# A linear-attention kernel feeding a SwiGLU block: diagonal blocks of the first group in 64x32 tiles, and joins over four array tiles in place of two

## The chip, the cores and the metric

The kernel runs on one core of one Trainium2 chip. The metric is the device time of one execution in microseconds (us); the time before is the median of three. A core has five engines that run side by side, each through its own queue in program order: TensorE (PE; matrix products, with a separate weight-load instruction, PEld), VectorE (DVE), ScalarE (ACT), GpSimd (POOL) and SyncE (SP, which here issues loads and stores). They wait for one another through semaphores. Data lies in SBUF, 128 partitions wide; PE writes its results into PSUM, and DVE or ACT copy them out.

## The reference, cut to what matters

```python
# q, k, v: (4, 8, 768, 48), beta: (4, 8, 768), all float32
k_n = k / (np.linalg.norm(k, axis=-1, keepdims=True) + 1e-06)
state = zeros((B, H, D, D))
for t in range(S):
    y[:, :, t] = q[:, :, t] @ state                  # per batch and head
    v_old = k_n[:, :, t] @ state
    state = state + beta_t * outer(k_n[:, :, t], v[:, :, t] - v_old)
x = y.transpose(0, 2, 1, 3).reshape(3072, 384)       # tokens, heads * head_dim
g, val = x @ w_gate, x @ w_val                       # (384, 1536) each
out = (g * sigmoid(g) * val) @ w_out                 # (1536, 384)
```

The recurrence over 768 steps is done in 12 chunks of 64 steps. In a chunk, the corrections of the steps on one another form a lower triangular system of 64 unknowns for each of the 32 (batch, head) pairs, made of the gram matrix of the chunk's keys and of beta. The kernel inverts that triangle. It treats two chunks at a time, called a group: group 0 is chunks 0 and 1. The two 32x32 diagonal blocks of every triangle are inverted on DVE by substitution, all 64 triangles of a group at once, one of the 128 blocks in each partition. The lower left block of the inverse is then a product of three 32x32 matrices, made on PE: this is the join.

## The kernel before: the parts that the change touches

Cuts are marked with `# ...`. C is 64 (steps in a chunk), R is 32, HH is 16 (heads side by side in a partition half), NB is 2, NJ is 4. All products are in float32; every float32 matmul is two records (a weight load and a matmul each) in the trace.

The gram matrix of a chunk, with its copies from PSUM to `a_sb`; the transposition of its diagonal blocks into `mb`; the substitution:

```python
def gram_steps(c, of_q, tag=None, copies=(nc.vector.tensor_copy,) * 2):
    xt = (qt if of_q else kt)[c]
    p_g = banks("p_g", tag or ("py" if of_q else "px"))
    p_v = [p.rearrange("p (bp j i) -> p bp j i", bp=NB, j=NJ) for p in p_g]
    for bp, j, par, b, _ in every():
        nc.tensor.matmul(
            p_v[par][half_of(b if of_q else b ^ par), bp, j],
            kt[c][half_of(par), bp, j, b],
            xt[half_of(par), bp, j, b],
        )
    if of_q:
        p_sb[c] = work.tile([128, 2, NB, NJ, C], FP32, name="p_sb", bufs=2)
    elif c % 2 == 0:
        a = work.tile([128, C * 2 * HH], FP32, name="a_sb")
        a_sb[c // 2] = (
            a.rearrange("p (i c h) -> p c h i", c=2, h=HH)
            if c == 0
            else a.rearrange("p (c h i) -> p c h i", c=2, h=HH)
        )
        a_of[c // 2] = a
    yield
    for par in range(2):
        p_h = p_g[par].rearrange("p (h i) -> p h i", i=C)
        if of_q:
            # ... masked product to p_sb
        else:
            at = slice(par * HH // 2, (par + 1) * HH // 2)
            copies[par](a_sb[c // 2][:, c % 2, at], p_h)
    yield
# ...
def turn(out, in_):
    nc.vector.transpose(out(slice(0, 128), 1), in_(slice(0, 128), 1))
    yield
    for rows in (slice(0, 32), slice(64, 96)):
        nc.vector.transpose(out(rows, 0), in_(rows, 0))
        yield
# ...
def scale_m(mb, m, b):
    zb = work.tile([128, R, R], FP32, name="zb", bufs=1)
    nc.gpsimd.memset(zb, 0.0)
    nc.gpsimd.tensor_copy(zb.rearrange("p k i -> p (k i)")[:, 0 : R * R : R + 1], b)
    nb = work.tile([128, R], FP32, name="nb", bufs=1)
    nc.vector.tensor_scalar_mul(nb, b, -1.0)
    for out, in_ in m:
        nc.vector.tensor_tensor(
            out=mb[:, out],
            in0=in_,
            in1=nb[:, None, :].to_broadcast([128, in_.shape[1], R]),
            op=ALU.mult,
        )
    return zb
def substitute(mb, zb):
    for j in range(R - 1):
        m = R - 1 - j
        tmp = work.tile([128, 256], FP32, name="tmp", bufs=1)
        t_v = tmp[:, 0 : (j + 1) * m].rearrange("p (k i) -> p k i", i=m)
        nc.vector.tensor_tensor(
            out=t_v,
            in0=zb[:, 0 : j + 1, j : j + 1].to_broadcast([128, j + 1, m]),
            in1=mb[:, j : j + 1, j + 1 : R].to_broadcast([128, j + 1, m]),
            op=ALU.mult,
        )
        nc.vector.tensor_tensor(
            out=zb[:, 0 : j + 1, j + 1 : R],
            in0=zb[:, 0 : j + 1, j + 1 : R],
            in1=t_v,
            op=ALU.add,
        )
        yield
```

The norms of the keys come as `n_t` from two powers on POOL; `first_n` turns them into factors, and `divide_beta` applies them twice to beta:

```python
def first_n():
    n = n_t[0].rearrange("p c h -> p (c h)")
    nc.vector.tensor_scalar_add(n, n, 1e-6)
    r_n = work.tile([128, R], FP32, name="r_n", tag="n_b", bufs=1)
    nc.vector.reciprocal(r_n, n)
    r_b = work.tile([128, R], FP32, name="r_b", tag="nb", bufs=1)
    nc.vector.transpose(r_b, r_n)
    return r_b
def divide_beta(g, r_n):
    for _ in range(2):
        nc.vector.tensor_tensor(
            out=beta_b[:, g], in0=beta_b[:, g], in1=r_n, op=ALU.mult
        )
```

After the substitution `late_z` writes the inverted blocks into `zt` and, turned, into `d_t`; `join_late` then makes the missing block. It is used for groups 0 and 1; later groups use another function, `join`, whose products are spread over four tiles of the array. `QUADS[n]` is the n-th quarter of the 128 partitions. The tile of the array that a matmul occupies follows from the partitions of its operands (rows) and of its result (columns).

```python
def late_z(g, zb):
    nc.vector.transpose(
        ztp[g % ZB].rearrange("p c h i -> p i (c h)")[:, R:C],
        zb.rearrange("p k i -> p i k"),
    )
    yield
    z_late[g] = work.tile([128, R, 2 * HH], FP32, name="d_t", tag="p_sb", bufs=2)
    nc.vector.transpose(z_late[g], zb)
    yield
def join_late(g, c, tags):
    zt, a, d_t = ztp[g % ZB], a_sb[g], z_late[g]
    p_j = banks("p_j", tags[0])[0].rearrange("p (h i) -> p h i", i=R)
    for h in range(HH):
        for s in range(2):
            hi, lo = QUADS[2 * s][0], QUADS[2 * s + 1][0]
            nc.tensor.matmul(p_j[hi, h], a[lo, c, h, 0:R], zt[lo, c, h, R:C])
    t2 = work.tile([128, HH, R], FP32, name="t2", tag="tmp", bufs=1)
    for s in range(2):
        hi = QUADS[2 * s][0]
        nc.scalar.mul(t2[hi], p_j[hi], -1.0)
    yield
    p_j = recur(ps_pair("p_j", tags[1]), C)
    for of_d in (True, False):
        for h in range(HH):
            par, bp, j = h // (NB * NJ), h // NJ % NB, h % NJ
            for s in range(2):
                hi = QUADS[2 * s][0]
                nc.tensor.matmul(
                    p_j[hi, par, bp, j, 0:R] if of_d else p_j[hi, par, bp, j, R:C],
                    d_t[hi, :, HH * c + h],
                    ident[hi, hi] if of_d else t2[hi, h],
                )
    zt_v = zt[:, c].rearrange("p (par bp j) i -> p par bp j i", par=2, bp=NB)
    for bp in range(NB):
        for hi in (QUADS[0][0], QUADS[2][0]):
            nc.scalar.copy(
                zt_v[hi, :, bp].rearrange("p par j i -> p par (j i)"),
                p_j[hi, :, bp].rearrange("p par j i -> p par (j i)"),
            )
    yield
```

The start of the program, in its order, which is the order of each engine's queue:

```python
# ... loads of k, beta, the first weights; norms(0), norms(1)
copy_a, copy_v = nc.scalar.copy, nc.vector.tensor_copy
turned(0, False)
turned(1, False, "py")
gram(0, False)
gram(1, False, "py", (copy_a, copy_v))
mb = new_mb()
a_v = a_of[0].rearrange("p (i m) -> p i m", i=C)
for _ in turn(
    lambda rows, half: mb[rows],
    lambda rows, half: a_v[rows, R * half : R * half + R],
):
    pass
r_b = first_n()
copy_v(beta_b, beta_s.rearrange("p (g r) -> p g r", g=NG)[:, :, 0:R])
for n in range(12, 17):
    stage(n)
load_v(1)
divide_beta(0, r_b)
zb = scale_m(mb, [(slice(0, R), mb)], beta_b[:, 0])
nc.gpsimd.memset(ztp[0], 0.0)
turned(0, True, "ffn")
turned(2, False, "px")
turned(3, False, "py")
first_q = gram_steps(0, True, "ffn")
next(first_q)
gram(2, False, "px", (copy_a, copy_a))
gram(3, False, "py", (copy_a, copy_a))
for n, _ in enumerate(substitute(mb, zb)):
    if n == R // 2:
        for i in range(4):
            power_step(i)
m_1 = turned_m(1, "ffn")
scale_v_heads(0)
turned(1, True, "px")
for _ in late_z(0, zb):
    pass
mb = new_mb()
mbs.append(mb)
first_join = join_late(0, 0, ("px", "py"))
next(first_join)
converts(2)
next(first_q)
next(first_join)
nc.scalar.copy(mb[:, m_1[0][0]], m_1[0][1])
step("advance", advance, 0)
converts(2)
step("advance", advance, 0)
nc.scalar.copy(mb[:, m_1[1][0]], m_1[1][1])
converts(2)
step("advance", advance, 0)
converts(2)
step("advance", advance, 0)
converts(2)
second_inverse.append(invert(1))
# ... then the gate and value products of chunk 0, with the second
# join of group 0 (join_late(0, 1, ...)) between the first of them
```

`converts` are the weights' conversions from float64 words to float32 on DVE and ACT, in pieces as they are loaded; `advance(0)` is the use of the inverted triangles for chunk 0, up to the input of the SwiGLU block.

## Time and profile before

| | |
|---|---|
| time, three runs | 747.40 (median), 746.36 to 749.35 us |
| span of the profiled run | 748.4 us |
| PE busy | 706.7 us, 10004 matmul records |
| DVE busy | 475.2 us, 981 instructions |
| ACT busy | 149.5 us |
| POOL busy | 67.4 us |
| first product of the SwiGLU block (L800) starts | 67.57 us |
| substitution of group 0 (L515, L521) | 23.63 to 47.6 us |
| joins of groups 0 and 1 (L568, L580) | at 49.8, 73.9, 180.3 and 198.8 us |

How to read it: a row of the timeline or of the groups gives the engine, the line of the kernel, the operation, then the tile written and the tiles read, the shape, and how often. Idle time ahead of an instruction stands in brackets with what ended it; "issue" there means that the engine waited for nothing that the profile shows. PEclk is the share of full clock that PE was granted. Busy shares of the whole span mix stages with different limits, so stages are read one by one.

### The profile page before, as it was taken

The page shows a single profiled execution, that of the slowest core. Times are in us where ns is not written, and L with a number is a line of the kernel's source. Part 1 is how long each engine was busy: PE and PEld are TensorE (multiplying, and loading weights), DVE is VectorE, ACT ScalarE, POOL GpSimd, SP SyncE. Part 2 cuts the span into 40 slices and gives each one's busy share as a digit, 9 for nine tenths or more (in the row PEclk, how much of TensorE's full clock was granted, in tenths as well). Part 3 has the DMA queues.
Part 4 walks back from the last instruction along what each step waited for, and adds up shares of the span by engine and source line. Part 5 has one row for each costly group of instructions (what it writes and reads, how often), then busy time and mean ns, then how long its engine had stood idle before and what let it go on. Part 6 is the DMA issues. An engine that isn't in the chain of part 4 may idle for free.

```text
span 748.4 us, 22217 instructions
## 1 busy us (share of the span) xinstructions
PE 706.7 (94%) x10004; PEld 614.1 (82%) x10004; DVE 475.2 (63%) x981; ACT 149.5 (20%) x277; POOL 67.4 (9%) x46
## 2 busy tenths in 40 slices
PE   4647999999999999999999999999999999999997
PEld 3536888866788688988888988988988988989987
DVE  5899888979368453478863478863478854223122
ACT  2346434211311111112011112011112011021010
POOL 7106200200300000030000030000030000000000
PEclk9755999999999999999999999999999999999999
DMA  7774534230203002231300331401220200000000
GB/s 154 184 213 109 148 68 124 64 53 23 55 14 50 16 16 32 47 61 34 54 14 17 49 61 28 57 10 24 42 46 2 43 3 3 22 3 0 22 1 21
DMA packets 130734, 37.17 MB, mean 50 GB/s; under 512 B 122864, under 2 KB 125936, under 8 KB 130640
## 3 DMA queue, kind: packets, MB, share of 16 engines
q1 hardware_dynamic: 127184, 34.01, 22.4%
q10 hardware_dynamic: 3072, 1.57, 1.0%
q8 instruction: 78, 1.28, 0.7%
q0 software_dynamic: 384, 0.17, 0.2%
q14 instruction: 16, 0.13, 0.1%
HBM read 31.01 MB, written 4.72 MB: 48 GB/s over the span
## 4 chain that ended last, share of the span: by engine, by line
PE 84%; DVE 10%; DMA 1%; issue 1%; SPq 1%; ACT 1%; ACTq 0%; DVEq 0%
PE p_gate L800 24%; PE p_val L800 23%; PE p_o L912 15%; PE p_o L829 6%; DVE tmp L515 3%; DVE zb L521 3%; PE p_g L444 2%; PE p_j L580 2%; PE p_y L735 2%; PE p_u L716 2%; PE p_s L747 2%; PE p_r L695 1%; PE p_y L704 1%; DVE h_f L870 1%; SPq L120 1%
## 5 line engine op out<-in xcount | busy, mean ns | idle before, releaser
L800 PE MATMUL p_gate<-x_ffn,wg_sb 128*128 128x256 f32 x864 | 208.3, 392 | 1.6 <-ACT x_ffn L783 1.6
L800 PE MATMUL p_val<-x_ffn,wv_sb 128*128 128x256 f32 x864 | 198.5, 379 | 0.0
L800 PEld LDWEIGHTS p_gate<-x_ffn,wg_sb 128*128 128x128 f32 x864 | 163.8, 194 | 25.4 <-ACT x_ffn L783 2.1
L800 PEld LDWEIGHTS p_val<-x_ffn,wv_sb 128*128 128x128 f32 x864 | 163.8, 190 | 22.3
L815 DVE TENSOR_TENSOR h_f<-sil,p_val 128x512 f32<-128x512 f32 x71 | 48.5, 684 | 152.4 <-PE p_val L800 151.9
L809 ACT ACTIVATE sil<-p_gate 128x512 f32<-128x512 f32 x72 | 43.0, 598 | 281.7 <-PE p_gate L800 258.1
L608 POOL TENSOR_TENSOR n_b<-mb,half 128x32 f32<-128x32 f32 x5 | 42.2, 8435 | 411.1 <-DVE mb L485 373.3
L912 PE MATMUL p_o<-wo_sb,h_f 128*128 128x192 f32 x432 | 75.6, 328 | 0.1
L515 DVE TENSOR_TENSOR tmp<-zb,mb 128x31 f32<-128x31 f32 (+15 forms) x186 | 63.2, 340 | 16.2 <-PE p_j L580 10.9
L912 PEld LDWEIGHTS p_o<-wo_sb,h_f 128*128 128x128 f32 x432 | 70.3, 190 | 1.2 <-DVE o_sb L922 0.7
L521 DVE TENSOR_TENSOR zb<-zb,tmp 128x31 f32<-128x31 f32 (+15 forms) x186 | 63.7, 342 | 6.4
L922 DVE TENSOR_TENSOR o_sb<-o_sb,p_o 128x192 f32<-128x192 f32 x45 | 15.7, 350 | 53.7 <-PE p_o L912 36.5
L829 PE MATMUL p_o<-wo_sb,h_f 128*128 128x384 f32 x136 | 45.7, 490 | 0.0
L829 PEld LDWEIGHTS p_o<-wo_sb,h_f 128*128 128x128 f32 x136 | 25.4, 190 | 16.5
L912 PE MATMUL p_o<-last_k,h_f 128*128 128x192 f32 x180 | 32.2, 326 | 0.0
L912 PEld LDWEIGHTS p_o<-last_k,h_f 128*128 128x128 f32 x180 | 29.7, 190 | 0.0
L870 DVE TENSOR_TENSOR h_f<-h_f,h_f 128x256 f32<-128x256 f32 x54 | 22.4, 424 | 8.0 <-PE p_o L912 7.1
L912 PE MATMUL p_o<-last_h,h_f 128*128 128x192 f32 x144 | 26.3, 326 | 0.0
L912 PEld LDWEIGHTS p_o<-last_h,h_f 128*128 128x128 f32 x144 | 23.9, 190 | 0.0
L254 ACT ACTIVATE last_h<-last_h,rebias 128x512 int32<-128x512 uint32 (+2 forms) x26 | 15.3, 616 | 31.8 <-DVE last_h L246 31.8
L485 DVE STREAM_TRANSPOSE mb<-a_sb 32x1024 f32<-32x1024 f32 x10 | 19.5, 1949 | 0.3
L716 PEld LDWEIGHTS p_u<-vin,zt 64*64 64x64 f32 x768 | 13.4, 141 | 6.1 <-issue 3.2
(163 smaller groups left out, 677.1 us busy)
## 6 DMA issues: line engine op xcount, KB each, us to landing
vin<-in_v_dram SPq DMA_DIRECT2D x96, 48.0 KB
kn<-in_k_dram SPq DMA_DIRECT2D x40, 96.0 KB
out_dram<-o_sb SPq DMA_DIRECT2D x36, 96.0 KB
zt<-in_moe_w_out_dram SPq DMA_DIRECT2D x6, 384.0 KB
staged<-in_moe_w_out_dram SPq DMA_DIRECT2D x6, 384.0 KB
qpad<-in_q_dram SPq DMA_DIRECT2D x36, 64.0 KB
wo_sb<-in_moe_w_gate_dram SPq DMA_DIRECT2D x4, 512.0 KB
wo_sb<-in_moe_w_val_dram SPq DMA_DIRECT2D x4, 512.0 KB
```

The source lines that it names most:

```text
L485: nc.vector.transpose(out(rows, 0), in_(rows, 0))
L515: nc.vector.tensor_tensor(out=t_v, in0=zb[:, 0 : j + 1, j : j + 1].to_broadcast([128, j + 1, m]), in1=mb[:, j : j + 1, j + 1 : R].to_broad ...
L521: nc.vector.tensor_tensor(out=zb[:, 0 : j + 1, j + 1 : R], in0=zb[:, 0 : j + 1, j + 1 : R], in1=t_v, op=ALU.add,)
L608: nc.gpsimd.tensor_tensor(out=n, in0=mb.rearrange("p j i -> p (j i)")[:, 0 : R * R : R + 1], in1=half, op=ALU.pow,)
L716: nc.tensor.matmul(p_u[half_of(b), par, bp, j], zt[half_of(b ^ par), par, bp, j], r[half_of(b ^ par), par, bp, j], start=first, stop=True, ...
L800: nc.tensor.matmul(ps[name][:, i], w_sb[:, t, (f + i) * 128 : (f + i + 1) * 128], xts[c][:, t], start=(t == 0), stop=(t == KT - 1),)
L809: nc.scalar.activation(sil, ps[name], ACTF.Silu)
L815: nc.vector.tensor_tensor(out=hs[c, f], in0=sil, in1=ps["p_val"], op=ALU.mult)
L829: nc.tensor.matmul(p_o, hs[c, f - f % 2][:, f % 2, bp * 128 : (bp + 1) * 128], wo_sb[:, f], start=(f == 0), stop=(f == FT - 1),)
L870: nc.vector.tensor_tensor(out=out, in0=a, in1=b, op=ALU.subtract)
L912: nc.tensor.matmul(p[x, part], a(f - f % 2)[:, f % 2], b(f), start=not begun and f == 0, stop=f == FH - 1, skip_group_check=True,)
L922: nc.vector.tensor_tensor(out=out, in0=a, in1=b, op=ALU.add)
```

## The change

Three things change, all in what is done for groups 0 and 1.

The gram matrices of chunks 0 and 1 are no longer made as 64x64 products. The upper left diagonal block is one 64x32 product (64 rows of the array, 32 columns), and the lower half, with the lower left and lower right blocks, another, so the two diagonal blocks of a triangle come out side by side in the same columns of PSUM. One copy for each half of the heads takes them all to one flat tile, and one transposition over all 128 partitions takes the place of three. The lower left blocks are copied apart.

The products of beta with the factors move to POOL, the copy of beta to ACT, and two memsets to DVE ahead of its first wait for data.

`join_late` sends even and odd heads to different tiles of the array, four in all in place of two. For that the odd heads' blocks are copied once more, into other partitions (`d_o`).

```diff
--- before.py
+++ after.py
@@ -450,12 +450,7 @@
             p_sb[c] = work.tile([128, 2, NB, NJ, C], FP32, name="p_sb", bufs=2)
         elif c % 2 == 0:
             a = work.tile([128, C * 2 * HH], FP32, name="a_sb")
-
-            a_sb[c // 2] = (
-                a.rearrange("p (i c h) -> p c h i", c=2, h=HH)
-                if c == 0
-                else a.rearrange("p (c h i) -> p c h i", c=2, h=HH)
-            )
+            a_sb[c // 2] = a.rearrange("p (c h i) -> p c h i", c=2, h=HH)
             a_of[c // 2] = a
         yield
         for par in range(2):
@@ -526,6 +521,55 @@
             )
             yield
 
+
+    first_of = {}
+
+    def first_tiles():
+        a = work.tile([128, C * 2 * HH], FP32, name="a_sb")
+
+        first_of["flat"] = a[:, 0 : R * R]
+        first_of["diag"] = a[:, 0 : R * R].rearrange("p (j h) -> p h j", j=R)
+        a_sb[0] = a[:, R * R :].rearrange("p (c h j) -> p c h j", c=2, h=HH)
+        zb = work.tile([128, R, R], FP32, name="zb", bufs=1)
+        nc.vector.memset(zb, 0.0)
+        nc.vector.memset(ztp[0], 0.0)
+        first_of["zb"] = zb
+
+    def first_gram(c, tag):
+
+        p_g = ps_pair("p_g", tag)
+        p_v = p_g.rearrange("p par (x h i) -> p par x h i", x=2, i=R)
+        for bp, j, par, b, _ in every():
+            k_v = kt[c][half_of(par), bp, j, b].rearrange("p (x i) -> p x i", x=2)
+            h, s_ = NJ * bp + j, b ^ par
+            hi, lo = slice(64 * s_, 64 * s_ + R), slice(64 * s_ + R, 64 * s_ + C)
+            nc.tensor.matmul(p_v[hi, par, 1, h], k_v[:, 0], k_v[:, 0])
+            nc.tensor.matmul(p_v[lo, par, :, h], k_v[:, 1], k_v)
+        return p_g, p_v
+
+    def first_diag(c, par, p, copy):
+        at = HH * c + HH // 2 * par
+        copy(first_of["diag"][:, at : at + HH // 2], p[1][:, par, 1])
+
+    def first_below(c, p):
+        for lo in (slice(R, C), slice(64 + R, 64 + C)):
+            nc.scalar.copy(
+                a_sb[0][lo, c].rearrange("p (par h) j -> p par (h j)", par=2),
+                p[0][lo, :, 0 : HH // 2 * R],
+            )
+
+    def first_scale(mb, r_b):
+        zb, b = first_of["zb"], beta_b[:, 0]
+        nb = work.tile([128, R], FP32, name="nb", tag="nb_1", bufs=1)
+        for _ in range(2):
+            nc.gpsimd.tensor_tensor(out=b, in0=b, in1=r_b, op=ALU.mult)
+        nc.gpsimd.tensor_copy(zb.rearrange("p k i -> p (k i)")[:, 0 : R * R : R + 1], b)
+        nc.vector.tensor_scalar_mul(nb, b, -1.0)
+        nc.vector.tensor_tensor(
+            out=mb, in0=mb, in1=nb[:, None, :].to_broadcast([128, R, R]), op=ALU.mult
+        )
+        return zb
+
     def recur(p, m=D):
         p = p[:, :, 0 : NB * NJ * m]
         return p.rearrange("p x (bp j d) -> p x bp j d", bp=NB, j=NJ)
@@ -560,35 +604,38 @@
 
     def join_late(g, c, tags):
 
+
         zt, a, d_t = ztp[g % ZB], a_sb[g], z_late[g]
-        p_j = banks("p_j", tags[0])[0].rearrange("p (h i) -> p h i", i=R)
-        for h in range(HH):
-            for s in range(2):
-                hi, lo = QUADS[2 * s][0], QUADS[2 * s + 1][0]
-                nc.tensor.matmul(p_j[hi, h], a[lo, c, h, 0:R], zt[lo, c, h, R:C])
-        t2 = work.tile([128, HH, R], FP32, name="t2", tag="tmp", bufs=1)
+        M = HH // 2
+        d_o = work.tile([128, M, R], FP32, name="d_o", tag="z1", bufs=1)
+        d_v = d_t[:, :, HH * c : HH * c + HH].rearrange("p k (m e) -> p e m k", e=2)
         for s in range(2):
-            hi = QUADS[2 * s][0]
-            nc.scalar.mul(t2[hi], p_j[hi], -1.0)
-        yield
-        p_j = recur(ps_pair("p_j", tags[1]), C)
+            nc.scalar.copy(d_o[QUADS[2 * s + 1][0]], d_v[QUADS[2 * s][0], 1])
+        p_j = banks("p_j", tags[0])[0][:, 0 : M * R].rearrange("p (m i) -> p m i", i=R)
+        for m in range(M):
+            for e in range(2):
+                for s in range(2):
+                    dst, lo = QUADS[2 * s + e][0], QUADS[2 * s + 1][0]
+                    h = 2 * m + e
+                    nc.tensor.matmul(p_j[dst, m], a[lo, c, h, 0:R], zt[lo, c, h, R:C])
+        t2 = work.tile([128, M, R], FP32, name="t2", tag="tmp", bufs=1)
+        nc.scalar.mul(t2, p_j, -1.0)
+        yield
+        p_j = ps_pair("p_j", tags[1]).rearrange("p e (m i) -> p e m i", i=C)
         for of_d in (True, False):
-            for h in range(HH):
-                par, bp, j = h // (NB * NJ), h // NJ % NB, h % NJ
-                for s in range(2):
-                    hi = QUADS[2 * s][0]
-                    nc.tensor.matmul(
-                        p_j[hi, par, bp, j, 0:R] if of_d else p_j[hi, par, bp, j, R:C],
-                        d_t[hi, :, HH * c + h],
-                        ident[hi, hi] if of_d else t2[hi, h],
-                    )
-        zt_v = zt[:, c].rearrange("p (par bp j) i -> p par bp j i", par=2, bp=NB)
-        for bp in range(NB):
+            for m in range(M):
+                for e in range(2):
+                    for s in range(2):
+                        row, hi = QUADS[2 * s + e][0], QUADS[2 * s][0]
+                        nc.tensor.matmul(
+                            p_j[hi, e, m, 0:R] if of_d else p_j[hi, e, m, R:C],
+                            d_o[row, m] if e else d_t[row, :, HH * c + 2 * m],
+                            ident[row, row] if of_d else t2[row, m],
+                        )
+        zt_v = zt[:, c].rearrange("p (m e) i -> p e m i", e=2)
+        for e in range(2):
             for hi in (QUADS[0][0], QUADS[2][0]):
-                nc.scalar.copy(
-                    zt_v[hi, :, bp].rearrange("p par j i -> p par (j i)"),
-                    p_j[hi, :, bp].rearrange("p par j i -> p par (j i)"),
-                )
+                nc.scalar.copy(zt_v[hi, e], p_j[hi, e])
         yield
 
     def invert(g):
@@ -1097,6 +1144,7 @@
         for at in range(0, 16, 2):
             load_beta(at)
             load_beta(at + 1, nc.sync)
+        first_tiles()
         norms(0)
 
         nc.vector.memset(places[0][:, 0:1], 0)
@@ -1115,23 +1163,23 @@
         copy_a, copy_v = nc.scalar.copy, nc.vector.tensor_copy
         turned(0, False)
         turned(1, False, "py")
-        gram(0, False)
-        gram(1, False, "py", (copy_a, copy_v))
+        p_g = [first_gram(0, "px"), first_gram(1, "py")]
+        first_diag(0, 0, p_g[0], copy_a)
+        first_diag(0, 1, p_g[0], copy_v)
+        copy_a(beta_b, beta_s.rearrange("p (g r) -> p g r", g=NG)[:, :, 0:R])
+        first_diag(1, 0, p_g[1], copy_a)
+        r_b = first_n()
+        first_diag(1, 1, p_g[1], copy_v)
         mb = new_mb()
-        a_v = a_of[0].rearrange("p (i m) -> p i m", i=C)
-        for _ in turn(
-            lambda rows, half: mb[rows],
-            lambda rows, half: a_v[rows, R * half : R * half + R],
-        ):
-            pass
-        r_b = first_n()
-        copy_v(beta_b, beta_s.rearrange("p (g r) -> p g r", g=NG)[:, :, 0:R])
+        nc.vector.transpose(
+            mb.rearrange("p j i -> p (j i)"), first_of["flat"]
+        )
         for n in range(12, 17):
             stage(n)
         load_v(1)
-        divide_beta(0, r_b)
-        zb = scale_m(mb, [(slice(0, R), mb)], beta_b[:, 0])
-        nc.gpsimd.memset(ztp[0], 0.0)
+        zb = first_scale(mb, r_b)
+        for c in range(2):
+            first_below(c, p_g[c])
 
         turned(0, True, "ffn")
         turned(2, False, "px")
```

## The prediction

> **What bounds the kernel now.** I read first the page (TensorE, PE, busy 706.7 us of a 748.4 us span), then the busy times in stages of my choosing, because the share of the whole span mixes two regimes.
>
> ```profile
> core 0: us, PE busy (x) PEld busy (x) DVE busy (x) ACT busy (x) POOL busy (x), PEclk, DMA share, GB/s
> 10.30:23.60 13.30, 8.59 (x153) 6.92 (x152) 11.04 (x17) 4.34 (x7) 6.93 (x5) 0.87 0.87 199
> 23.60:47.70 24.10, 9.68 (x459) 8.50 (x457) 21.94 (x66) 9.48 (x28) 0.55 (x1) 0.67 0.81 232
> 67.50:86.00 18.50, 18.43 (x290) 15.64 (x291) 16.12 (x34) 9.18 (x16) 11.80 (x1) 0.78 0.69 202
> 86.00:112.00 26.00, 25.29 (x473) 21.73 (x472) 22.66 (x41) 9.60 (x16) 0.00 (x0) 1.00 0.30 72
> 112.00:180.00 68.00, 68.00 (x467) 52.63 (x465) 58.87 (x138) 16.50 (x30) 4.78 (x5) 1.00 0.30 70
> 180.00:211.00 31.00, 30.31 (x759) 24.22 (x758) 15.12 (x26) 9.79 (x17) 7.34 (x3) 0.97 0.20 41
> ```
>
> Until 67.5 us PE is less than half busy and VectorE (DVE) sets the pace; from there on PE is all but full. So a microsecond taken from the early DVE chain, or from PE after 67.5 us, should reach the end one for one, provided the other engine doesn't take over. The timeline of DVE, idle time and its releaser in brackets, shows the early chain:
>
> ```profile
> 12.38 1.88 DVE L472 COPY a_sb<-p_g 128x512 f32<-128x512 f32 x2 [0.41 <-PE p_g L444]
> 15.14 1.01 DVE L472 COPY a_sb<-p_g 128x512 f32<-128x512 f32 x1 [0.87 <-ACT a_sb L472]
> 16.18 1.25 DVE L482 STREAM_TRANSPOSE mb<-a_sb 128x1024 f32<-128x1024 f32 x1
> 17.46 2.48 DVE L485 STREAM_TRANSPOSE mb<-a_sb 32x1024 f32<-32x1024 f32 x2
> 19.97 0.18 DVE L386 TENSOR_SCALAR n_t<-n_t 128x32 f32<-128x32 f32 x1
> ...
> 21.34 0.26 DVE L1128 COPY beta_b<-wo_sb 128x192 f32<-128x192 f32 x1 [0.55 <-DMA last_k<-in_k_dram]
> 21.63 0.42 DVE L369 TENSOR_TENSOR beta_b<-beta_b,r_b 128x32 f32<-128x32 f32 x2
> 22.09 0.18 DVE L500 TENSOR_SCALAR nb<-beta_b 128x32 f32<-128x32 f32 x1
> 22.30 1.23 DVE L502 TENSOR_TENSOR mb<-mb,nb 128x1024 f32<-128x1024 f32 x1
> 23.63 0.19 DVE L515 TENSOR_TENSOR tmp<-zb,mb 128x31 f32<-128x31 f32 x1
> ```
>
> The substitution starts at 23.63 and its 62 dependent operations keep DVE until 47.6, when the first join begins. The 0.55 us before L1128 is not the last_k load: that source line's view has eight semaphore events of DVE's queue from 20.6 to 21.2, which wait for the sixteen beta loads one pair after another. It is a cost of waiting as such.
>
> The joins, from the timeline of PE (columns: start, length, then tile and count):
>
> ```profile
> 51.63 1.15 PE L580 MATMUL p_j<-ident,d_t 32*32 32x32 f32 x32
> 53.93 0.94 PE L580 MATMUL p_j<-ident,d_t 32*32 32x32 f32 x25 [1.16 <-issue]
> ...
> 180.26 1.20 PE L568 MATMUL p_j<-zt,a_sb 32*32 32x32 f32 x64
> 182.88 2.00 PE L580 MATMUL p_j<-ident,d_t 32*32 32x32 f32 x64
> 184.72 1.99 PE L580 MATMUL p_j<-t,d_t 32*32 32x32 f32 x64
> ...
> 261.22 1.29 PE L659 MATMUL p_j<-zt,a_sb 32*32 32x32 f32 x128
> ```
>
> The last row is the join of a later group, written for four distinct 32x32 tiles: 128 records in 1.29 us, about 10 ns each. L568 alternates two tiles and takes 1.20/64, about 19 ns each; L580 about 31.
>
> **What the Trainium skill says.** "TensorEngine Tiling (Array Packing)", section Tiling Modes, says that different tiles execute weight loads and matmuls in parallel, with 8 tiles in a 64x32 configuration and 16 in 32x32. The trace agrees: L659 against L568 above is a factor of two in rate for twice the tiles. "TensorE: Matmul & The Clock Gate", section Back-to-back issue gap, gives 25 ns as the floor per small matmul; the 10 ns of L659 are below it, so I take 10. "SBUF — State Buffer", section "Door 1: The DMA port swizzle", says that consecutive accesses want to fall in the same 16-byte line. The trace agrees where a_sb is written with a stride: 1.01 us at 15.14 on DVE, against 682 ns as the median of the fifteen copies of L472 there. "Runtime: NRT & Kernel Launch", section Instruction fetch mechanics, says instructions come in 16 KiB blocks of 256, mostly hidden. Here the fetch is not always hidden: PE stands for 2.94 us at 29.52, 0.54 at 33.52, 2.48 at 38.07 and 1.16 at 53.93, labelled issue, and counted in its instructions these places are multiples of 256 apart.
>
> **The change part by part.**
>
> 1. Gram matrices of the first group. Before: 128 records of 64x64 from 10.33 to 14.02, about 28.8 ns each (mean, slower than the 18 of the same matmuls at 24 us, 1.16 us for 64). After: twice as many, 256 records, in eight tiles. If the 10 ns of four tiles hold, times 28.8/18 for the same early slowness, that is 16 ns each and 4.1 us: about break-even, end at 14.4. But 512 PE instructions now lie where 256 lay. From the spacing of the issue stalls one block ends after about 77 records of the first gram and the next at about record 205. From the stall at 53.93: PE resumed at 49.80 after a long wait, and again after fetching at 53.93, 4.1 us later. With the first boundary crossed at 10.33 + 77 x 0.016 = 11.6, the block is there at 15.7, where PE would have needed it at 13.6. I put the stall at 2.1 us, and the end of the second gram at 15.7 + 51 x 0.016 = 16.5.
>
> 2. From the grams to the substitution. Removed from DVE: three 512-wide strided copies, two extra transposes (2.48), the beta copy with its 0.55 of waits, two multiplications, and most of the dependence on order. Left after the second gram: a diagonal copy on ACT, 256 wide and strided, half of 1.02, so 0.5; the same on DVE behind it, 0.5; one transpose 1.25; nb 0.18; the scaling of mb 1.23; five hand-overs at about 0.1. That is 3.66 + 0.5 = 4.2 us. The norm chain (POOL's two powers end at 14.95, then 0.8 on DVE) is done at 15.8 and fits in before. POOL's two beta products and the diagonal of zb (0.24 for one such 128x32 copy in the trace, so 0.8 in all) run beside DVE's copy and transpose. Substitution at 16.5 + 4.2 = 20.7, against 23.63: **-2.9 us**. Without the fetch stall it would be -4.9, limited to about -4.5 by the norm chain, the copy and the transpose behind it.
>
> The two memsets (zb, zt) go from POOL to DVE ahead of its 5.27 us wait for the first keys: hidden. Four below-diagonal copies on ACT (32x512, 0.58 each, 2.3 us) fall before the copies of q: PE waits there for loads anyway, so hidden.
>
> 3. First join, c=0, on the path. L568 took 2.0 us at half clock; on four tiles 1.0. New: two copies into d_o on ACT (32x256 with a strided source, taken as 0.5 each), which hold the second half until about 2.0 us after zt; one scaling of t2 (0.6) instead of two (1.20). The second half's 128 records go from 31 to 16 ns. But the fetch at 53.93 counts from PE's resumption, 4.1 us after it, with 89 records still to go: 89 x 15 ns = 1.35 us saved. The copies to zt now come by even and odd heads, so most of p_u waits for the last of them: I take 0.35 back. **-1.0 us**.
>
> 4. First group, c=1, 73.9 to 82.4 us, PE bound. 1.0 from L568 and about 1.8 from L580, but DVE converts weights without rest here. Its only idle times for PE between 67 and 96 us are 2.31 at 78.69 and 0.39 at 90.86, and at 96.27 PE waits 0.71 for DVE. PE can gain on DVE at most 2.31 + 0.39 = 2.7 in all, of which part 3 uses 1.0: **-1.7 us**, where PE alone would give 2.8.
>
> 5. Second group, two joins, 180 to 210 us. Each saves 0.6 from L568 and 1.8 from L580: 4.8. The second L568 is followed by a 0.61 us wait for ACT's x_ffn, which grows by what L568 saves: -0.6. From L568 at 180.26 to the end of L735 at 196.4 PE works off 528 records, 3.9 us for each block of 128 (a record is a weight load and a matmul, so 256 instructions), already about the 4.1 us of a fetch: what is made faster here may wait for instructions, and I take another 0.9 back, a choice and not a reading. **-3.3 us**.
>
> Sum: -2.9 - 1.0 - 1.7 - 3.3 = -8.9; 747.4 - 8.9 = 738.5 us.
>
> **Rivals.**
>
> - *Instructions become the bound.* The change adds 256 PE instructions early and makes the joins faster than blocks can be fetched. For it: the issue stalls above. Against: none shows where 64x64 matmuls are mixed with long ones. If it takes half of parts 1, 3 and 5: 742.
> - *Eight 64x32 tiles don't overlap as four do.* If a 64-row group takes the same time per record whatever its columns (28.8 ns per record as before), the grams take 256 x 28.8 ns = 7.4 us and end at 17.7; the substitution gains only 1.7 and the total is 739.7. Against: L659 uses only two row groups with four column groups and still runs at 10 ns.
> - *DVE does not bind in 67 to 96 us.* Then part 4 gives 2.8 and, with no stall in part 1, all goes right: 747.4 - 4.5 - 1.5 - 2.8 - 4.8 = 733.8.
> - *Loads bind.* Weights are consumed earlier by 4 to 6 us; the queue has 87% DMA share in 10 to 24 us. Against: DVE shows no idle time for a weight load between 67 and 112 us. Cost if so: 2 to 3 us.
>
> **Range and chances.** Every part saves in some measure, so slower needs a new wait of a kind not seen. The rivals span 733.8 to 742, and the clock grants (PEclk 0.50 to 0.78 until 86 us) can move it by a microsecond or two. I give 735 to 742.5 for 8 in 10. Two per cent is 732.5, below the best case worked out: 0.04 faster, 0.94 same, 0.02 slower.
>
> **What would show it.** In the changed profile: 256 records on the first p_g near 16 ns with an issue stall in the second gram; the first substitution near 20.7; records of the joins at 10 to 16 ns; DVE's idle times at h_f before 96 us gone and PE's wait for vin there longer; PE busy about 5 to 7 us lower. It is wrong if the grams run above 25 ns a record, if the joins stay near 31, or if PE opens gaps after 112 us.

## The result and the profile after

The changed kernel takes 738.44 us (median; 738.12 to 739.26), the kernel before 747.56 us on the same chip (746.36 to 749.35): a ratio of 0.9878, 95% interval 0.9856 to 0.9899. The prediction was 738.5. In a later group of runs it took 738.56 us against 748.72, ratio 0.9860 (0.9845 to 0.9874). The gain is thus 9 to 10 us, and the rest of this text asks which term of the sum it came from, because a right total can be made of wrong terms.

The page's first part, of after:

```profile
PE 697.5 (95%) x10132; PEld 604.7 (82%) x10132; DVE 473.1 (64%) x977; ACT 154.7 (21%) x287; POOL 66.9 (9%) x46
```

PE is busy 9.2 us less than before (706.7) with 128 records more, where the prediction had 5 to 7 us. Of the 9.2, 3.9 belong to matmuls that the change does not touch, the 864 of p_gate (one of the two input products of the SwiGLU block), here in the page's fifth part of before and of after:

```profile
L800 PE MATMUL p_gate<-x_ffn,wg_sb 128*128 128x256 f32 x864 | 208.3, 392 | 1.6 <-ACT x_ffn L783 1.6
L847 PE MATMUL p_gate<-x_ffn,wg_sb 128*128 128x256 f32 x864 | 204.4, 387 | 1.5 <-ACT x_ffn L830 1.5
```

Fewer of them fell into stretches of half clock, which the experiments come back to. The joins that were changed, PE's matmuls into p_j up to 215 us, are busy 21.7 us before and 12.5 after. So p_gate and the joins together are 13 us less busy, and what remains, for the most part early matmuls at half clock, is some 4 us more. DVE is all but unchanged.

The chain of waits of after, from the grams to the substitution (start, length, what):

```profile
12.96 2.90 issue
...
16.77 0.60 ACT a_sb L552
17.39 0.60 DVE a_sb L552
18.02 1.25 DVE mb L1174
19.26 0.07 DVE nb L567
19.36 1.24 DVE mb L568
```

The 2.90 us stand between two records of the second gram that wait for no other engine. The scaling at 19.36 is followed by the substitution, at 20.69; it began at 23.63 before.

PE's timeline of after, in the first group's second join, the end of that stage, and the second group (start, length, line, operation, tile, count, and in brackets the idle time before with what ended it):

```profile
74.24 0.24 PE L630 MATMUL p_j<-ident,d_o 32*32 32x32 f32 x2 [0.95 <-ACT d_o L613]
...
90.45 1.15 PE L763 MATMUL p_u<-vin,zt 64*64 64x48 f32 x64 [1.23 <-DVE vin L759]
...
174.45 0.75 PE L620 MATMUL p_j<-zt,a_sb 32*32 32x32 f32 x64
...
191.35 0.75 PE L620 MATMUL p_j<-zt,a_sb 32*32 32x32 f32 x64 [0.54 <-DVE state L803]
192.63 2.86 PE L847 MATMUL p_gate<-x_ffn,wg_sb 128*128 128x256 f32 x12 [0.52 <-ACT x_ffn L830]
```

64 records of L620 on four tiles take 0.75 us, where L568 took 1.20 on two: about 12 ns each in place of 19. PE now waits for ACT's copies into `d_o` (0.95 us), and more than before for DVE at L763 (1.23 in place of 0.71). In the second group, two waits of half a microsecond stand ahead of the next p_gate. In DVE's timeline of before, the product of sil and p_val had idle time ahead of it twice in this stage; then the first of the two in after:

```profile
78.69 0.69 DVE L815 TENSOR_TENSOR h_f<-sil,p_val 128x512 f32<-128x512 f32 x1 [2.31 <-PE p_val L800]
...
90.86 0.69 DVE L815 TENSOR_TENSOR h_f<-sil,p_val 128x512 f32<-128x512 f32 x1 [0.39 <-PE p_val L800]
```

```profile
73.33 0.68 DVE L862 TENSOR_TENSOR h_f<-sil,p_val 128x512 f32<-128x512 f32 x1
```

No bracket: DVE no longer waits there, nor anywhere between 67 and 94 us. The stages, from the start of each in the profiles of before, of after, and of after profiled again (zt is the tile of the inverted triangles, into which DVE transposes when the substitution is done):

| stage, us | before | after | again |
|---|---|---|---|
| start to the first zt transposes (after the substitution) | 47.74 | 44.75 | 44.07 |
| from there to p_u(1), the product L763 of chunk 1 | 48.52 | 45.70 | 45.72 |
| from there to the end | 652.1 | 647.1 | 647.0 |

The three rows are less by 3.0, 2.8 and 5.1 us, 10.9 in all, where the prediction had 2.9, 2.7 (parts 3 and 4) and 3.3. The medians differ by 9.1 only: the profiled execution of before was one of its slowest, 750.13 us, where its four timed runs took 746.36 to 749.35. A difference of these two profiles is thus about 2 us too large as a whole.

### The profile page after: what moved, and what is told of

It is laid out like the page before. It is cut to its first block, busy times and chain, and to the rows that moved or that the text cites. A ratio compares the mean times of both kernels' runs of the same rounds, so it can differ in the third digit from the quotient of the medians.

```text
span 737.5 us, 22478 instructions
## 1 busy us (share of the span) xinstructions
PE 697.5 (95%) x10132; PEld 604.7 (82%) x10132; DVE 473.1 (64%) x977; ACT 154.7 (21%) x287; POOL 66.9 (9%) x46
## 3 DMA queue, kind: packets, MB, share of 16 engines
q8 instruction: 79, 1.29, 0.7%
## 4 chain that ended last, share of the span: by engine, by line
PE 83%; DVE 14%; issue 1%; DMA 1%; ACT 0%; ACTq 0%; SPq 0%; DVEq 0%
PE p_gate L847 23%; PE p_val L847 23%; PE p_o L959 17%; PE p_o L876 6%; DVE tmp L510 3%; PE p_g L444 3%; DVE zb L516 3%; PE p_u L763 2%; PE p_r L742 1%; PE p_s L794 1%; PE p_y L782 1%; PE p_y L751 1%; DVE last_h L287 1%; PE p_t L432 1%; DVE h_f L862 1%
## 5 line engine op out<-in xcount | busy, mean ns | idle before, releaser
L847 PE MATMUL p_gate<-x_ffn,wg_sb 128*128 128x256 f32 x864 | 204.4, 387 | 1.5 <-ACT x_ffn L830 1.5
L847 PEld LDWEIGHTS p_gate<-x_ffn,wg_sb 128*128 128x128 f32 x864 | 161.1, 191 | 24.2 <-ACT x_ffn L830 2.0
L876 PEld LDWEIGHTS p_o<-wo_sb,h_f 128*128 128x128 f32 x136 | 25.3, 190 | 16.5
L763 PEld LDWEIGHTS p_u<-vin,zt 64*64 64x64 f32 x768 | 13.7, 141 | 6.9 <-issue 3.2
L763 PE MATMUL p_u<-vin,zt 64*64 64x48 f32 x768 | 15.7, 228 | 2.4 <-DVE vin L759 1.2
```

Of the source, the lines that this page charges most:

```text
L763: nc.tensor.matmul(p_u[half_of(b), par, bp, j], zt[half_of(b ^ par), par, bp, j], r[half_of(b ^ par), par, bp, j], start=first, stop=True, ...
L847: nc.tensor.matmul(ps[name][:, i], w_sb[:, t, (f + i) * 128 : (f + i + 1) * 128], xts[c][:, t], start=(t == 0), stop=(t == KT - 1),)
L876: nc.tensor.matmul(p_o, hs[c, f - f % 2][:, f % 2, bp * 128 : (bp + 1) * 128], wo_sb[:, f], start=(f == 0), stop=(f == FT - 1),)
```

## The experiments

Each kernel is compared with runs of the kernel before on the same chip: 748.83 us for the first four of the table, 748.72 for the next four, 748.42 for the last four. In the diffs, `+` and `-` are against the changed kernel unless something else is said.

| kernel | median, us | ratio to before (95%) |
|---|---|---|
| grams only | 744.59 | 0.9934 (0.9913 to 0.9955) |
| joins only | 741.55 | 0.9899 (0.9883 to 0.9916) |
| second group on two tiles | 745.01 | 0.9945 (0.9923 to 0.9966) |
| fetch early | 741.39 | 0.9890 (0.9867 to 0.9913) |
| the changed kernel again | 738.56 | 0.9860 (0.9845 to 0.9874) |
| fetch early, norms last | 739.84 | 0.9874 (0.9857 to 0.9890) |
| odd blocks early | 739.34 | 0.9868 (0.9852 to 0.9885) |
| scaling on GpSimd | 740.44 | 0.9881 (0.9866 to 0.9896) |
| scaling on ACT | 738.38 | 0.9870 (0.9845 to 0.9895) |
| fetch early, norms between | 740.64 | 0.9887 (0.9859 to 0.9916) |
| both of these | 737.59 | 0.9862 (0.9833 to 0.9890) |
| both, and a store moved | 737.55 | 0.9852 (0.9833 to 0.9871) |

**One half of the change at a time.** First the new grams with the old joins, then (against the kernel before) the new joins with the old grams.

```diff
     # first_tiles, first_gram, first_diag, first_scale: as changed
     # join_late:
-        for m in range(M):
-            for e in range(2):
-                for s in range(2):        # ... four tiles, with d_o
+        for h in range(HH):
+            for s in range(2):            # ... two tiles, as before
```

> The changed start (64x32 grams, one transpose, beta on the other engines), with the joins of before on two tiles. Theory (the parts add up): the substitution starts at 20.7 us as in the changed kernel, and the 2.9 us pass through the busy DVE and PE to the end one for one: 744.6 us, ratio 0.996. Rival (the early gain is given back where weights are converted or loaded): 746.5 to 747.5, with new idle time of DVE or PE for a load between 60 and 112 us.

```diff
     # against the kernel before; gram and the transposes: as there
     # join_late:
-        for h in range(HH):
-            for s in range(2):            # ... two tiles
+        for m in range(M):
+            for e in range(2):
+                for s in range(2):        # ... four tiles, with d_o
```

> The start of before, with the joins of groups 0 and 1 on four tiles. Theory: the substitution at 23.6 us as before; 2.8 us from group 0 (the idle time of DVE that PE can use up, whatever PE saves beyond it) and 4.0 from group 1, so 740.7 us. Rival (the joins gain only what PE saves in records, with nothing bound by DVE): 2 x 2.4 from group 1 and 3.5 to 4 from group 0, 738.7. Rival (the joins are worth little by themselves, their gain needs the earlier start): 745.

744.59 and 741.55 us, against 744.6 and 740.7 expected. As differences from the kernel before on the same chip (748.83) the grams alone bring 4.2 us and the joins alone 7.3; their sum of 11.5 is a little more than the 10.2 of both together in the repeat, so that the two parts nearly add up. Both are somewhat larger than the prediction's parts for them (2.9, and 1.0 + 1.7 + 3.3 = 6.0), with intervals of some 1.5 us each way. In the grams-only profile the substitution starts at 19.48 us, 4.15 earlier than in before, and not at the expected 20.7: the stall in the second gram is 1.97 us long there and not 2.90, with the same start of the program.

**The second group back on two tiles.**

```diff
-            yield from join_late(1, c, ("px", "py"))
+            yield from join_late_two(1, c, ("px", "py"))   # the join of before
```

> The changed kernel, with the joins of group 1 alone put back on two tiles. Theory: group 1 is worth 4.0 us, read from how far the same matmuls moved between the two profiles (5.8 us ahead of it, 9.8 behind), so 742.4 us. Rival (part of the 9.8 is a half-clock window that the profile before happened to have at 209 us): 3.0 or less, 741.4. A half-clock window behind the 3.75 us burst of the second join would speak for a cause of it in the burst.

745.01 us, where 742.4 was expected: 6.4 us more than the changed kernel (738.56) in place of 4.0, and the prediction had 3.3; from p_u(1) to the end its profile takes 653.9 us, against 647.1. The second group is thus worth more than predicted. In the profiles of before and after, the joins themselves, from the start of the first to the p_gate behind the second, differ by 4.0 us (29.48 and 25.50); what lies behind them differs by another 1.1. Where that is, the timelines of PE show, of before and of after, the second half of the second join and the next p_gate:

```profile
205.96 2.00 PE L580 MATMUL p_j<-ident,d_t 32*32 32x32 f32 x64
207.80 2.01 PE L580 MATMUL p_j<-t,d_t 32*32 32x32 f32 x64
209.74 4.19 PE L800 MATMUL p_gate<-x_ffn,wg_sb 128*128 128x256 f32 x12
```

```profile
199.95 2.86 PE L847 MATMUL p_gate<-x_ffn,wg_sb 128*128 128x256 f32 x12
```

The join's half takes 3.8 us from 205.96 to the next p_gate before, and 1.9 after (198.01 to 199.95): that was foreseen. The same twelve matmuls of p_gate then take 4.19 us before and 2.86 after. PE's granted clock is one half for 3.4 us from 209.0 in before, and full in after from 67.3 us to the last microsecond; so 1.3 us of the gain in this pair of profiles came from the clock. In this kernel, with two tiles, such windows came twice in the second group (180.8 and 204.7; p_gate at 204.77 took 4.49), in the grams-only kernel once (180.2). With four tiles they came in the second group in two of eleven profiles, both told of below, and behind 67 us in the first group in four of twelve; before has one there too, at 82.8.

The Trainium skill says in "TensorE: Matmul & The Clock Gate", section What's actually happening, that the clock is set by windows of about 3.4 us that run freely, and that a window in which PE is idle brings half clock. The length agrees with the trace. But in before PE was busy in the 3.4 us ahead of 209.0, with the 128 matmuls of 32x32 from 205.96 to 209.74. In the grams-only kernel the stretch is 176.98 to 180.76, ahead of the window at 180.2. In the second group two-tile halves last 3.8 us, longer than a window; four-tile halves last 1.9. So it seems that a window filled mostly with 32x32 matmuls or with waiting counts as idle. The fourteen profiles bear this out, from 65 us on: all eight full-clock windows in which such matmuls and waiting took 80% or more of the time were followed by half clock, three of the ten with 67 to 76%, and none with less. Why the ten differ isn't shown, and no run changes the share alone.

**Fetching early.** 37 small matmuls, whose results nobody reads, ahead of the first transposes, while PE waits for keys: they shift what follows against the instruction blocks.

```diff
+        p_d = ps_ffn([128, 512], "p_d")
+        for n in range(37):
+            nc.tensor.matmul(p_d[0:R, R * (n % 16) : R * (n % 16) + R], half, half)
```

> The changed kernel, with 37 small matmuls on a constant tile put ahead of the first transposes, where PE stands idle; their results are not used. They move the boundaries of PE's instruction blocks by 148, so that the block which the second gram waited for is asked for before the grams begin. Theory: the 2.9 us issue stall at 12.96 falls to 1.5 or less and the grams end near 15.2 in place of 16.7, but the norm chain (POOL's powers end at 16.2) then holds DVE, so the substitution starts at 20.3 in place of 20.7: 738.1 us. Rival (the stall is of another cause): it stays 2.9 us. Rival (the stall alone sets the start): substitution at 19.2 and 736.9.

The stall at its old place in the second gram is gone, and a shorter one lies two records into that gram, in PE's timeline of this kernel:

```profile
12.55 0.21 PE L547 MATMUL p_g<-kt 64*32 64x64 f32 x1 [1.67 <-issue]
```

Both stand ahead of the 222nd weight load of PE's program, after record 204 of the grams in the changed kernel and after record 130 here. So it belongs to the place in the program and not to the data; in all twelve profiles with the new grams it stands ahead of this weight load. The boundary before it was crossed earlier, while PE waited for keys, which would make it shorter. The grams take 4.7 us in place of 6.4, and the substitution starts at 19.54, against 20.69 and (repeat) 20.04. The chain of waits now runs over GpSimd's two powers, 6.5 us, up to 15.53: the norm chain is next. The grams-only kernel, without the 37 matmuls, has its powers done at 15.34 and starts the substitution at 19.48; so 19.54 lies within what the stall and the arrival of the keys do by themselves. And the time is 2.8 us above the changed kernel's in the next group. What took it is told with the third try of this kind, below.

**The changed kernel again**, as reference:

> The changed kernel itself, once more, as the reference of this group. Both theories: 0.9878 of the kernel before, so 9.1 us less, within 1.5 us. What may differ from the first time is where windows of half clock fall (none past 67 us the first time): each such window of 3.4 us may cost up to 1.7 us.

738.56, and again no half clock between 67.5 us and the last microsecond. Its stall is 2.52 us long and its substitution starts at 20.04.

**DVE's order behind the early fetch.**

```diff
+        # 37 small matmuls as above
         first_diag(1, 0, p_g[1], copy_a)
-        r_b = first_n()
         first_diag(1, 1, p_g[1], copy_v)
         # ... transpose of a_sb to mb
+        r_b = first_n()
```

> The changed kernel with 37 small matmuls ahead of the first transposes, so that the block boundary falls into a wait for loads, and with DVE's last diagonal copy and the transpose ahead of its norm chain. Theory (the fetch stall and then the norm chain hold the substitution): grams end at 13.8, transpose of a_sb done near 16.2, norms and beta done at 17.8, scaling 1.25 behind them: substitution at about 19.2 against 20.69, so 1.5 us less than the changed kernel. Rival (DVE's order does not matter, the norm chain alone sets it): 19.5 as with the early fetch alone, 1.15 us less. Rival 2 (a front won is lost again later): substitution near 19.3, but the time within 0.5 us of the changed kernel.

The theory falls: substitution at 20.37, later than with the early fetch alone. The norm chain behind the transpose begins at 17.30, although its powers were there at 15.6; GpSimd's products with beta and the scaling then follow at 18.21 and 19.04. The chain that was thought hidden now sets the end.

**Does DVE bound the stage up to p_u(1)?** Three tries: PE faster, DVE relieved by GpSimd, DVE relieved by ACT. First, the two copies into `d_o` for the first group's second join are issued ahead of the join:

```diff
             nc.scalar.copy(d_o[QUADS[2 * s + 1][0]], d_v[QUADS[2 * s][0], 1])
+        if g == 0 and c == 1:
+            yield
         # ... where the second join is made:
+        next(second)
```

> The changed kernel with the two copies into d_o of the first group's second join made on ACT well before the join, so that PE no longer waits 0.95 and 0.42 us for them. Theory (DVE bounds 67 to 96 us): PE reaches L763 1.3 us earlier and waits there as much longer for DVE's vin (1.23 becomes about 2.5); start of p_u(1) after the first zt transposes stays 45.7 +- 0.3, the time within 0.4 us of the changed kernel. Rival (PE bounds this stage): p_u(1) 1.3 us earlier, the time 1.3 us less, wait for vin unchanged.

738.56 became 739.34: nothing gained. PE has no wait for `d_o` left in this join, and from the start of the join's second half to the next p_gate it takes 1.9 us (73.62 to 75.56) where the repeat took 3.5. And then, in the timelines of PE and of ACT of this kernel:

```profile
80.27 1.16 PE L444 MATMUL p_g<-qt,kt 64*64 64x64 f32 x64 [1.86 <-ACT zt L640]
```

```profile
76.66 1.34 ACT L254 ACTIVATE last_h<-last_h,rebias 128x512 int32<-128x512 uint32 x2 [3.51 <-DVE last_h L246]
77.90 2.32 ACT L640 COPY zt<-p_j 32x512 f32<-32x512 f32 x4
```

PE's gain became a wait of 1.86 us (0.34 in the repeat of the changed kernel) for the copies to `zt`. ACT makes these in program order behind two conversions of weights, which stood 3.51 us waiting for DVE. So the theory is right that DVE gives the time; the place of the wait was foreseen at the wrong line (L763 instead of the p_g of L444), because ACT's order carries DVE's lateness to PE. DVE itself had 0.98 us of idle time in this run, waiting for p_val at 73.73: the issue stall in the first join was longer here (1.65 us, 1.11 in the repeat), and PE was at half clock until 69.1 us in place of 67.5. p_u(1) starts 46.73 us after the zt transposes, 1.0 later than in the repeat, and that is this idle time.

Second, the scaling of `vin` of chunk 1 on GpSimd:

```diff
-        nc.vector.tensor_tensor(out=r, in0=r, in1=n, op=ALU.mult)
+        engine = nc.gpsimd if c == 1 else nc.vector
+        engine.tensor_tensor(out=r, in0=r, in1=n, op=ALU.mult)
```

> The changed kernel with one 0.95 us multiplication of the stage 60 to 96 us moved from DVE to GpSimd. Theory (DVE bounds 67 to 96 us): DVE reaches the vin copy about 0.95 us earlier, PE's wait there falls from 1.23 to about 0.3, start of p_u(1) after the first zt transposes 44.8 instead of 45.7, and the time about 0.9 us less than the changed kernel. Rival (PE bounds it): no change of p_u(1), time within 0.3 us; or, if GpSimd's multiplication ends after the copy that needs it, up to 2 us more.

1.9 us worse than the changed kernel. The timelines of DVE and GpSimd of this run show the price of the move:

```profile
76.00 1.70 DVE L246 TENSOR_SCALAR last_h<-zt 128x512 uint32<-128x512 uint32 x1
```

```profile
75.47 1.94 POOL L402 TENSOR_TENSOR vin<-vin,n_t 128x768 f32<-128x768 f32 x1
```

While GpSimd multiplies (1.94 us for what DVE does in 0.95), one operation of DVE that takes 0.42 elsewhere takes 1.70. The 0.95 us taken from DVE come back as 1.28 of slowing, a loss of 0.3. The Trainium skill says in "SBUF — State Buffer", section Who interferes with whom, that the two engines share a pair of ports which, where both need it, the first to come holds for its whole instruction. The trace agrees: the DVE operation ends 0.3 us after GpSimd's, at 77.7, and the lock is seen as a longer operation, not as a wait.

The rest of the 1.9 us lies elsewhere in this profile. DVE waits 0.92 us for p_val(0,0), behind an issue stall of 2.19 us in the first join. ACT's copies to `zt`, behind conversions that wait for DVE, come late, so that PE waits 2.59 us ahead of the p_g of L445 (0.34 in the repeat, there L444); half clock from 81.8 to 85.2 follows, and at p_u(1) PE is last and not DVE. So this run tells what the move costs, and not whether DVE bounds the stage.

Third, the same on ACT, in sixteen pieces, one for each head, placed into ACT's idle time ahead of 87 us:

```diff
                 fill(2)
+                if (c, f) == (0, 2):
+                    scale_v_heads(1)          # 16 scalings of 128x48 on ACT
         # ... advance
-        if c > 0:
+        if c > 1:
             scale_v(c)
```

> The changed kernel with the scaling of vin for the first group's second chunk (0.95 us on DVE) done on ACT, in 16 pieces of about 0.23 us that fit into ACT's 4.6 us of idle time ahead of 87 us. Theory (DVE bounds the stage from the substitution to p_u(1)): DVE reaches the subtraction of p_r 0.95 us earlier, PE's wait for it falls from 1.23 to about 0.3, and p_u(1) starts 44.75 us after the first zt transposes plus DVE's idle time before it, where the kernels so far took 45.7 plus that idle time; the time 0.9 us less than the changed kernel, 737.6. Rival (PE bounds it): 45.7 as before, the time within 0.3 us of 738.5.

p_u(1) starts 45.13 us after the zt transposes: 0.57 of the 0.95. In this run PE did not wait for DVE at L763 at all, because PE's clock was halved from 76.8 to 80.2 us:

```profile
76.46 4.54 PE L847 MATMUL p_gate<-x_ffn,wg_sb 128*128 128x256 f32 x12
```

Twelve matmuls take 4.54 us instead of 2.86, and so PE became the bound here. The time, 738.38, can't be told from the changed kernel's.

What DVE gives is seen best over the profiles together: the time from the zt transposes to p_u(1), and DVE's idle time in it (left out are the scaling on GpSimd and on ACT alone, where PE was the bound).

| kernel | DVE idle, us | zt to p_u(1), us | difference |
|---|---|---|---|
| before | 2.70 | 48.52 | 45.82 |
| grams only | 1.08 | 46.83 | 45.75 |
| joins only | 0 | 45.88 | 45.88 |
| second group on two tiles | 0.20 | 45.97 | 45.77 |
| after / again | 0 | 45.70 / 45.72 | 45.70 / 45.72 |
| fetch early | 0.37 | 46.14 | 45.77 |
| fetch early, norms last | 0 | 45.66 | 45.66 |
| odd blocks early | 0.98 | 46.73 | 45.75 |
| fetch early, norms between | 1.29 | 47.05 | 45.76 |
| scaling on ACT, with early fetch and norms between | 0 | 44.62 | 44.62 |
| the same, store moved | 0.32 | 45.01 | 44.69 |

With the same work on DVE, the difference is 45.66 to 45.88 in ten profiles, whatever joins PE runs, and in each of them PE waits 0.7 to 1.2 us for DVE at p_u(1); with 0.95 us less on DVE it is 44.6 to 44.7, a difference of 1.1. DVE is the bound, and PE matters through how late p_val(0,0) comes, or, as just seen, where its clock is halved.

**Early fetch with the norm chain between copy and transpose, and both together.**

```diff
+        # 37 small matmuls as above
         first_diag(1, 0, p_g[1], copy_a)
-        r_b = first_n()
         first_diag(1, 1, p_g[1], copy_v)
+        r_b = first_n()
         # ... transpose of a_sb to mb
```

> The changed kernel with the 37 small matmuls ahead of the first transposes, and on DVE the last diagonal copy, then the norm chain, then the transpose. Theory (the fetch stall, then GpSimd's two powers and the norm chain, hold the substitution; what the last try lost was the transpose ahead of the norm chain): norms done at about 16.4, transpose 17.6, scaling of mb 19.0, substitution at 19.1, 0.9 to 1.5 us earlier than in the two profiles of the changed kernel (20.0 and 20.7). The time 0.9 less, 737.6, if DVE gets no idle time for p_val(0,0) in exchange. Rival (what the front gains is lost as DVE's idle time at p_val, because ACT's and PE's part between is not faster): substitution at 19.1, and the time within 0.3 us of 738.5.

The substitution starts at 19.06, as expected, 1.0 us earlier than in the repeat. p_gate(0,0), the first product of the SwiGLU block, starts at 63.02, where the repeat has 63.07: the whole gain is gone, and DVE then waits 1.29 us for p_val. It went in the first join, where PE's timeline has a stall labelled issue of 1.98 us at 50.97 (1.11 at 50.26 in the repeat). Such a stall is not a fixed tax: at the same place the next kernel, with the same front, has 0.35 us. Why it differs isn't shown. And the second group, in the timelines of ACT's queue and ACT, and of PE, of this kernel:

```profile
190.75 2.23 ACTq L893 DMA_DIRECT2D out_dram<-o_sb  x2
193.02 0.80 ACT L830 COPY x_ffn<-p_f 128x768 f32<-128x768 f32 x1 [2.31 <-DMA out_dram<-o_sb]
```

```profile
193.87 4.54 PE L847 MATMUL p_gate<-x_ffn,wg_sb 128*128 128x256 f32 x12 [1.98 <-ACT x_ffn L830]
```

ACT issues two stores ahead of the `x_ffn` copy. That took 2.23 us here, 1.99 in the first early-fetch kernel and 1.31 in after; PE waited 1.98, 1.50 and 0.52 us for `x_ffn`. In these two kernels a window of half clock followed that wait (the 3.4 us ahead of it hold mostly the wait and the 32x32 matmuls of L620), and p_gate took 4.54 us instead of 2.86. These two things are 2.7 to 3.1 us of the 3.3 that both lost from p_u(1) to the end (650.3 and 650.4 against 647.1), and most of the reason why in these profiles an earlier start gave a later end. (The profile of this kernel is of its slowest execution, 742.17 us; the fastest took 739.06.) Why the issue took longer in these two isn't shown.

With both edits:

> The two edits before together (scaling on ACT; early fetch with the norm chain between). Theory: they act on two parts of one chain of DVE and add up: 1.8 us less than the changed kernel, 736.7. Rival (the earlier DVE only waits longer for p_val): as the better of the two alone, 737.6.

And with the store of chunk 1 issued by GpSimd:

```diff
-            (nc.scalar if c < FAST else nc.sync).dma_start(
+            (nc.gpsimd if c == 1 else nc.scalar if c < FAST else nc.sync).dma_start(
```

> The kernel with both edits, and the store of the second chunk's output issued by GpSimd instead of ACT, whose issue of 1.31 us ahead of the x_ffn copy makes PE wait 0.52 us for x_ffn in the second group. Theory: that wait goes, 0.5 us less than with both edits, 736.2. Rival: the wait for DVE's state or another takes its place, within 0.2 us.

Both together: the substitution at 18.76, PE's wait for DVE at L763 is 0.16 us, and the profiled execution, the fastest of the four, spans 735.0 us, 1.8 less than the repeat. The medians are 737.59 and 737.55, where 736.7 and 736.2 were expected, and about 1 us below the changed kernel's, which was measured on another chip; the intervals overlap with its own. Both are 1.4 to 1.5% faster than before; that they are faster than the changed kernel is not shown. With the store moved, PE's waits ahead of the second group's first p_gate are gone, and p_u(1) to the end takes 647.1 us in place of 647.6; the medians don't tell the two apart.

## Why the prediction was right, point by point

1. *Grams.* The boundary was put at about record 205 of the grams; the stall stands after record 204. The grams start at 9.98 and not 10.33, and records take 13.6 ns, not 16 (the first 204 in 2.76 us), so that PE reached the boundary at 12.74 and not at 13.6, and the next block came at 15.86, not 15.7: a longer stall (2.9 us, not 2.1) made up for the faster records. The grams end at 16.74; 16.5 was the prediction. That this profile comes so near is partly luck: in the seven profiles with this start the stall is 1.97 to 2.90 us long and the grams end at 15.53 to 16.74, the latest in this one. Eight tiles do overlap: that rival is out.
2. *Grams to substitution.* 20.69 against 20.7, and the terms are as worked out: copies of 0.6 each, not 0.5, the transpose 1.25, the scaling 1.23. From the end of the grams to the substitution all seven profiles take 3.95 us, 4.2 in the prediction; with the end of the grams, the substitution moves between 19.48 and 20.69. One step was wrong without harm in this version: GpSimd's powers end at 16.17 and not at 14.95 (they start 0.57 later and take 6.51 us in place of 5.86), so the norm chain "fits in before" by a hair only. It is done at 17.0, just under the copy, and it is the bound once the stall is shortened.
3. *First join.* From the zt transposes to p_gate(0,0), 0.5 us less in after (19.30) and 0.8 in the repeat (19.00) than in before (19.83), not 1.0. The copies into `d_o` take 0.63 each and not 0.5, and PE waits for them; the fetched block came 4.4 us after PE's resumption (46.82 to 51.23), where 4.1 was expected. That stall is what varies, from under 0.3 to 2.19 us. Without it, the stretch takes 17.9 to 18.0 us in all twelve profiles with four tiles here, and 18.7 and 18.5 in the two with two tiles: the join gave 0.5 to 0.8 us, and the fetch decides the rest.
4. *Chunk 1 of the first group.* The step that carries this part, "PE can gain on DVE at most 2.31 + 0.39 = 2.7 in all, of which part 3 uses 1.0", is what the runs confirm best: 2.8 us, DVE's idle time gone, and the table above. The wait for vin grew only from 0.71 to 1.23, since half of what PE gained stayed in a new wait of 0.95 and 0.42 us for `d_o`.
5. *Second group.* The term that was mis-sized most: 3.3 predicted, 5.1 in the profiles, 6.4 from the medians of the two-tile experiment (which had two windows of half clock in it). The 0.9 us for instruction fetching, called a choice, isn't there: in after no stall labelled issue stands between 180 and 210 us, and the joins' four pieces save 0.45, 1.81, 0.53 and 1.84, 4.6 in all. The 0.6 us taken off for `x_ffn` are there under another name: a new wait of 0.54 us for DVE's state, ahead of the second join. The 1.3 us on top are the window of half clock in before, which no step had.

So the total came out within 0.1 us of the median because part 5 was taken nearly 2 us too low, while the profile from which all was worked out was some 2 us slower than the median that the sum was taken from: two errors of one size, against one another, which is luck. The range of 735 to 742.5 is the better statement of what was known. Of the rivals, "instructions become the bound" was half right: it is so in the front, not in the second group. "DVE does not bind" is out by the table above. "Loads bind" is out: DVE has no idle time for a load in the stage up to p_u(1) in any of these profiles.

## What to carry to other kernels

Before making one engine faster, write down the idle time of the engine that it feeds. Where that engine bounds the stage, this is all there is to gain (here 2.7 us of DVE's idle time, and a gain of 2.8), and the order of a third engine between them decides at which line the rest comes back as a wait. A stall that sits at a fixed place in the instruction stream falls on other work when instructions are added ahead of it, and shortening it is worth no more than the slack of the next chain (here the norms; the best of these tries started the substitution 1.0 to 1.4 us earlier than the repeat). Such a stall also differs from one profile to the next by as much as the gain that is looked for, so a stage that holds one is compared over several profiles. And a gain of 1 us at the front is not safe until the end of the trace: look for the half-clock window, the store issue and the block boundary behind it.

## What the runs showed of the hardware that was not expected

- The matmuls on 64x32 tiles ran at 13.6 ns a record, where those on 64x64 tiles at the same place in the program before took 28.8.
- The stall at one block boundary, the 222nd weight load, lasted 1.97 to 2.90 us in seven profiles with the same instructions ahead of it.
- PE's clock fell to half in windows of 3.4 us in the middle of the kernel, after 3.4 us filled mostly with 32x32 matmuls or with waiting; twelve dense matmuls that take 2.86 us took 4.19 to 4.54 us in such a window.
- The issue of the same two stores by ACT took 1.31 (the changed kernel), 1.99 and 2.23 us in three kernels.
- GpSimd's multiplication of 128x768 elements lengthened a DVE operation from 0.42 to 1.70 us.
